# A value product as Strassen's seven block products over pairs of 384 tokens, in three phases via DRAM

## The chip, the cores and the metric

The kernel runs on one core of one Trainium2 chip. The metric is the device time of one execution in microseconds (us), and the lower it is the better. The core's engines are TensorE (PE in the profile, with its weight loads as PEld), VectorE (DVE), ScalarE (ACT), GpSimd (POOL) and SyncE (SP, which issues the DMAs here).

## What is computed

Three blocks follow one another: causal attention with a cumulative decay, a gated spatial block (the first block, moe1 in the code) and a channel-mixing block (the last block). The change is in the last one:

```python
def _moe2_ref(x, mu_k, mu_r, w_k, w_v, w_r):
    x_prev = concatenate([zeros((B, 1, D)), x[:, :-1, :]], axis=1)
    xk = mu_k * x + (1.0 - mu_k) * x_prev
    xr = mu_r * x + (1.0 - mu_r) * x_prev
    k = np.maximum(xk @ w_k, 0.0)
    v = k * k @ w_v                       # 1024 -> 512, the value product
    r = 1.0 / (1.0 + np.exp(-(xr @ w_r))) # the gates
    return r * v
```

There are 4 x 576 = 2304 tokens, the width is 512 and the inner width 1024.

## The kernel before, in words

Every product runs in float32r with operands split in two: a high part (hi, a ScalarE copy to float32r) and the rest (lo, one VectorE subtraction, `split_lo`, line 66). A product of two numbers is then three matmuls, hi x hi, hi x lo and lo x hi, summed in PSUM (`gemm3`, line 355). The weights come as 64-bit words, and `convert` (lines 71 to 88) makes two float32r tiles of them with ScalarE and VectorE passes.

The code is written for a scheduler that runs a timeline model when the program is built: it orders the instructions of each engine by priority (the order of writing) among those that are ready in the model. The order in each queue is thus fixed when the chip runs it; every engine, and SP with its DMAs, takes its instructions in that order. `after(late, early)` adds an edge for that order alone.

Attention (`attn_pair`) and the first block (`moe1`, lines 359 to 465) overlap: `attention_until` interleaves them. The first block's stages are called v, u, sg (the gates ga, split into gh and gl) and o; o leaves y, which lines 464 and 465 store to DRAM twice, in `ydram[0]` as it is and in `ydram[1]` shifted by a token, so that x and x_prev of the last block can be loaded as two rows of one tile.

The last block works on chunks of 512 tokens (the fifth has 256), all stages of a chunk before the next chunk:

- `late(i)` (line 549) loads and converts a slice of w_k (0 to 7), w_r (8 to 11) or w_v (12 to 19).
- `prep(c)` (line 560) loads `yt` and mixes x and x_prev with mu on ScalarE (line 569) and VectorE (line 570), then splits the results, for k (tiles vn0, vn1) and for r (xs0, xs1).
- the k stage (lines 588 to 602): 8 output blocks of 128 rows, each 12 matmuls of 512 columns, then Relu on ScalarE (599), square on VectorE (600), and the split into kh and kl (601, 66). These stay in SBUF.
- `gate(m)` (line 605): 4 blocks, 12 matmuls each, and a Sigmoid on ScalarE.
- the value product, "vo" in the trace (lines 620 to 629): 4 blocks, each 24 matmuls (8 slices of the inner width, 3 matmuls each), then one VectorE pass that multiplies with the gate, and a store to the output.

The PSUM pool `psum1` has all 8 banks (tags sc, tp, acc), and `bank` deals them out in turn. GpSimd works in attention and the first block and has nothing to do in the last block.

Of the kernel before, what the change touches and what calls it, by code (L numbers as in the profile page):

```python
# [37 lines left out]
def fused_kernel(ctx, tc, kqT, vL, s, w_in, g_ln, w_sgT, b_sg, w_out, mu_k, mu_r, w_k, w_v, w_r, out):  # L38
# [52 lines left out]
    psum1 = ctx.enter_context(tc.tile_pool(name="psum1", bufs=3, space=bass.MemoryType.PSUM))  # L91
    ew = ctx.enter_context(tc.tile_pool(name="ew", bufs=1))
    ep = ctx.enter_context(tc.tile_pool(name="ep", bufs=1))
    ap_stack = ExitStack()
    at = ap_stack.enter_context(tc.tile_pool(name="at", bufs=2))
# [9 lines left out]
    wv = [ew.tile([P, KD, FH], F32R, tag=f"wv{i}", name=f"wv{i}") for i in range(2)]  # L105
# [35 lines left out]
    def prologue():  # L141
        st = []
        for i in range(KD + 3):
            if i % 2 == 0:
                raw = ep.tile([P, KD, S], F32, tag="xs0", name=f"sraw{i}")
# [213 lines left out]
    def moe1(b):  # L359
# [5 lines left out]
        xs = [ep.tile([P, KD, S], F32R, tag=f"xs{i}", name=f"xs{i}_{b}") for i in range(2)]  # L365
# [62 lines left out]
        for m in range(KD):  # L428
# [15 lines left out]
            nc.scalar.copy(gs[0][m], ga[:, :S])  # L444
            gs[1].append(ep.tile([P, S], F32R, tag="u", name=f"gl{b}_{m}", bufs=4))
            split_lo(eng, gs[1][m], ga[:, :S], gs[0][m])
        for m in range(KD):
# [19 lines left out]
    exps = []  # L467

# [71 lines left out]
    lw = ctx.enter_context(tc.tile_pool(name="lw", bufs=1))  # L540
    wk = [lw.tile([P, KD, DFF], F32R, tag=f"wk{i}", name=f"wk{i}") for i in range(2)]
    wr = [lw.tile([P, KD, DM], F32R, tag=f"wr{i}", name=f"wr{i}") for i in range(2)]
    wva = [ew.tile([P, KD, FH], F32R, tag=f"wv{i}", name=f"wva{i}") for i in range(2)]
    wvb = [ew.tile([P, NT, S], F32R, tag=f"wsg{i}", name=f"wvb{i}") for i in range(2)]
    wvv = [[wva[i][:, k] for k in range(KD)] + [wvb[i][:, k, :DM] for k in range(KD)] for i in range(2)]
    loads = [(w_k[k * P:(k + 1) * P, j * 512:(j + 1) * 512], [t[:, k, j * 512:(j + 1) * 512] for t in wk]) for j in range(2) for k in range(KD)]
    loads += [(w_r[k * P:(k + 1) * P], [t[:, k] for t in wr]) for k in range(KD)]
    loads += [(w_v[k * P:(k + 1) * P], [t[k] for t in wvv]) for k in range(KF)]
    def late(i):
        src, (hi, lo) = loads[i]  # L550
        raw = lw.tile([P, 512, 2], U32, tag="lraw", name=f"lraw{i}", bufs=2)
        nc.sync.dma_start(out=raw.rearrange("p n c -> p (n c)"), in_=src.bitcast(U32))
        y = lw.tile([P, 512], F32, tag="ltmp", name=f"ly{i}", bufs=4)
        t = lw.tile([P, 512], F32, tag="ltmp", name=f"lz{i}", bufs=4)
        convert(hi, lo, raw, y[:, :512], t[:, :512].bitcast(U32), nc.vector, low=mhalf[:, 0:1])

    CH = 512
    TOK = B * S

    def prep(c):  # L560
        n = min(CH, TOK - c * CH)
        t0 = c * CH
        xx = [[ep.tile([P, KD, S], F32R, tag=t, name=f"x{t}_{c}") for t in r] for r in (("vn0", "vn1"), ("xs0", "xs1"))]
        for k in range(KD):
            yt = lw.tile([P, 2, CH], F32, tag="yt", name=f"yt{c}_{k}", bufs=2)
            nc.sync.dma_start(out=yt[:, :, :n], in_=ydram[:, k, :, t0:t0 + n].rearrange("i p n -> p i n"))
            for r in range(2):
                t = lw.tile([P, CH], F32, tag="ltmp", name=f"lt{c}_{k}_{r}", bufs=4)[:, :n]
                nc.scalar.mul(t, yt[:, 1, :n], mu[:, r, 1, k:k + 1])
                nc.vector.scalar_tensor_tensor(out=t, in0=yt[:, 0, :n], scalar=mu[:, r, 0, k:k + 1], in1=t, op0=ALU.mult, op1=ALU.add)  # L570
                nc.scalar.copy(xx[r][0][:, k, :n], t)
                split_lo(nc.vector, xx[r][1][:, k, :n], t, xx[r][0][:, k, :n])
        return xx

    for c in range((TOK + CH - 1) // CH):
        n = min(CH, TOK - c * CH)
        t0 = c * CH
        if c == 0:
            for i in range(8):
                late(i)  # L580
        xk, xr = prep(c)
        if c == 0:
            for i in range(8, 12):
                late(i)
        kh = [ep.tile([P, S], F32R, tag="xT", name=f"kh{c}_{m}", bufs=8) for m in range(KF)]
        kv = ep.tile([P, KD, S], F32R, tag="v", name=f"kl{c}")
        kk = [kh, [kv[:, m] for m in range(KD)] + [ep.tile([P, S], F32R, tag="u", name=f"kl{c}_{m}", bufs=4) for m in range(KD, KF)]]
        for m in range(KF):
            f = slice(m * P, (m + 1) * P)
            if c == 0:  # L590
                late(12 + m)
            t = ep.tile([P, S + 1], F32, tag="tmp", name=f"lk{c}_{m}", bufs=3)[:, :n]
            acc = bank(f"k{c}_{m}")
            mms = []
            for k in range(KD):
                xh, xl = (x[:, k, :n] for x in xk)
                mms += [(wk[0][:, k, f], xh), (wk[0][:, k, f], xl), (wk[1][:, k, f], xh)]
            gemm3(acc[:, :n], mms)
            nc.scalar.activation(t, acc[:, :n], AF.Relu, scale=1.0 / WS)  # L599
            nc.vector.tensor_tensor(out=t, in0=t, in1=t, op=ALU.mult)  # L600
            nc.scalar.copy(kk[0][m][:, :n], t)
            split_lo(nc.vector, kk[1][m][:, :n], t, kk[0][m][:, :n])
        sg = {}

        def gate(m):
            f = slice(m * P, (m + 1) * P)
            sg[m] = ew.tile([P, S], F32, tag="wc", name=f"sg{c}_{m}", bufs=3)[:, :n]
            acc = bank(f"r{c}_{m}")
            mms = []
            for k in range(KD):  # L610
                xh, xl = (x[:, k, :n] for x in xr)
                mms += [(wr[0][:, k, f], xh), (wr[0][:, k, f], xl), (wr[1][:, k, f], xh)]
            gemm3(acc[:, :n], mms)
            nc.scalar.activation(sg[m], acc[:, :n], AF.Sigmoid, scale=1.0 / WS)

        gate(0)
        for m in range(KD):
            if m + 1 < KD:
                gate(m + 1)
            f = slice(m * P, (m + 1) * P)  # L620
            o = ep.tile([P, S + 1], F32, tag="tmp", name=f"o{c}_{m}", bufs=3)[:, :n]
            acc = bank(f"vo{c}_{m}")
            mms = []
            for k in range(KF):
# [52 lines left out]
```

## Time and profile before

| | us |
|---|---|
| median of 3 runs (706.54 to 709.41) | 708.18 |
| the profiled execution's own time | 706.47 |
| its span, from the first to the last instruction | 704.5 |
| TensorE busy | 668.2 |
| VectorE busy | 438.4 |
| ScalarE busy | 396.0 |
| GpSimd busy | 210.8 |

All rows below come from the one profiled execution. The span is divided into 40 slices of 17.6 us; a digit is the busy share of a slice in tenths. Matmuls are pipelined, so the time of one in a row (0.39 us, say) is longer than the distance from one to the next; the distance is got from the starts of two groups. Attention and the first block take about the first 450 us, the last block the rest.

### The profile page before, as it was taken

The page shows a single profiled execution, that of the slowest core. Times are in us where ns is not written, and L with a number is a line of the kernel's source. Part 1 is how long each engine was busy: PE and PEld are TensorE (multiplying, and loading weights), DVE is VectorE, ACT ScalarE, POOL GpSimd, SP SyncE. Part 2 cuts the span into 40 slices and gives each one's busy share as a digit, 9 for nine tenths or more (in the row PEclk, how much of TensorE's full clock was granted, in tenths as well). Part 3 has the DMA queues.
Part 4 walks back from the last instruction along what each step waited for, and adds up shares of the span by engine and source line. Part 5 has one row for each costly group of instructions (what it writes and reads, how often), then busy time and mean ns, then how long its engine had stood idle before and what let it go on. Part 6 is the DMA issues. An engine that isn't in the chain of part 4 may idle for free.

```text
span 704.5 us, 11476 instructions
## 1 busy us (share of the span) xinstructions
PE 668.2 (95%) x4000; PEld 556.6 (79%) x4000; DVE 438.4 (62%) x996; ACT 396.0 (56%) x899; POOL 210.8 (30%) x219
## 2 busy tenths in 40 slices
PE   2779989999998999999999999999999999999998
PEld 2446767878976889977988899888888888888898
DVE  7876589995578555478743489898744445344140
ACT  5777787874557554368743387598544245234130
POOL 8445555368246258236364140000000000000000
PEclk9979999999999999999999999999999999999999
DMA  7763551542743332743400884753602301100100
GB/s 224 210 194 101 157 153 50 174 146 78 228 149 99 113 84 61 247 122 99 127 18 23 306 301 165 261 175 116 185 25 75 93 13 45 60 16 0 39 22 31
DMA packets 39049, 84.30 MB, mean 120 GB/s; under 512 B 4752, under 2 KB 10384, under 8 KB 38992
## 3 DMA queue, kind: packets, MB, share of 16 engines
q1 hardware_dynamic: 38992, 83.57, 38.1%
q8 instruction: 32, 0.52, 0.3%
q14 instruction: 25, 0.20, 0.1%
HBM read 55.55 MB, written 18.50 MB: 105 GB/s over the span
## 4 chain that ended last, share of the span: by engine, by line
PE 80%; DVE 11%; DMA 3%; ACT 2%; issue 2%; POOL 1%; SPq 0%; DVEq 0%; ACTq 0%; POOLq 0%
PE k L355 14%; PE vo L355 14%; PE pv L326 8%; PE r L355 7%; PE sg L355 7%; PE v L355 6%; PE o L355 6%; PE tp L296 4%; PE sc L247 4%; PE u L355 4%; PE sc L248 3%; DVE st L272 1%; DVE QB L224 1%; DMA lraw<-in_w_k_dram 1%; DMA sraw<-in_w_in_dram 1%
## 5 line engine op out<-in xcount | busy, mean ns | idle before, releaser
L355 PE MATMUL k<-xvn,wk 128*128 128x512 f32 (+1 forms) x480 | 102.0, 373 | 0.3 <-DVE y L461 0.3
L355 PEld LDWEIGHTS k<-xvn,wk 128*128 128x128 f32 x480 | 83.6, 188 | 17.7 <-DVE y L461 0.5
L280 ACT ACTIVATE st<-st,mx 128x128 f32<-128x128 f32 (+4 forms) x124 | 72.3, 585 | 31.2 <-DVE mx L272 29.7
L247 PE MATMUL sc<-ka,qa 128*128 128x512 f32 (+3 forms) x180 | 64.0, 366 | 21.9 <-ACT wv L84 10.6
L272 DVE CUSTOM_DVE_ANT_0 st<-sc,mask 128x512 f32<-128x512 f32 (+3 forms) x124 | 61.0, 501 | 15.6 <-PE sc L248 13.0
L326 PE MATMUL pv<-pt,vf 128*64 128x320 f32 (+4 forms) x448 | 66.7, 375 | 1.3 <-DVE u L485 1.2
L355 PE MATMUL sg<-wsg,vn 128*128 128x288 f32 x448 | 65.0, 298 | 1.2 <-DVE u L485 1.2
L247 PEld LDWEIGHTS sc<-ka,qa 128*128 128x128 f32 x180 | 33.5, 187 | 36.9 <-DVE mx L272 16.0
L355 PEld LDWEIGHTS sg<-wsg,vn 128*128 128x128 f32 x448 | 60.5, 188 | 2.5 <-DVE u L485 1.5
L66 POOL TENSOR_TENSOR KB<-kq,ka 64x576 fp32r<-64x576 f32 x29 | 43.7, 1509 | 50.0 <-ACT ka L225 27.3
L248 PE MATMUL sc<-KB,QB 128*128 128x512 f32 (+3 forms) x180 | 58.2, 336 | 0.2 <-DVE QB_f L224 0.2
L326 PEld LDWEIGHTS pv<-pt,vf 128*64 128x64 f32 x448 | 35.6, 140 | 27.5 <-issue 6.8
L355 PE MATMUL r<-xxs,wr 128*128 128x512 f32 (+1 forms) x240 | 53.4, 373 | 0.0
L66 POOL TENSOR_TENSOR qa<-kq,QB 64x576 fp32r<-64x576 f32 x29 | 43.3, 1493 | 31.0 <-DVE QB L224 17.3
L296 PE MATMUL tp<-ident,st 128*128 128x128 f32 x300 | 48.7, 281 | 3.3 <-ACT st L280 1.7
L599 ACT ACTIVATE lk<-k 128x512 f32<-128x512 f32 (+1 forms) x40 | 22.2, 557 | 51.9 <-PE k L355 48.5
L355 PE MATMUL vo<-kh,wva 128*128 128x512 f32 (+1 forms) x160 | 49.0, 369 | 0.0
L355 PE MATMUL vo<-kh,wvb 128*128 128x512 f32 (+1 forms) x160 | 48.8, 368 | 0.0
L355 PEld LDWEIGHTS r<-xxs,wr 128*128 128x128 f32 x240 | 42.0, 188 | 8.5
L628 DVE SCALAR_TENSOR_TENSOR o<-vo,sg 128x512 f32<-128x512 f32 (+1 forms) x20 | 12.6, 636 | 57.9 <-PE vo L355 57.9
L355 PE MATMUL v<-wv,xs 128*128 128x512 f32 x192 | 48.1, 396 | 0.0
L296 PEld LDWEIGHTS tp<-ident,st 128*128 128x128 f32 x300 | 35.9, 143 | 8.0 <-ACT st L280 2.8
(174 smaller groups left out, 1466.8 us busy)
## 6 DMA issues: line engine op xcount, KB each, us to landing
wc<-wscr SPq DMA_DIRECT2D x24, 512.0 KB
kq<-in_kqT_dram SPq DMA_DIRECT2D x32, 288.0 KB
ydram<-y SPq DMA_DIRECT2D x32, 288.0 KB
yt<-ydram SPq DMA_DIRECT2D x16, 512.0 KB
vf<-in_vL_dram SPq DMA_DIRECT2D x16, 320.0 KB
qa<-QB SPq DMA_DIRECT2D x30, 144.0 KB
ka<-ka SPq DMA_DIRECT2D x30, 144.0 KB
wscr<-wcs SPq DMA_DIRECT2D x8, 512.0 KB
```

The source lines that it names most:

```text
L66: eng.tensor_tensor(out=lo, in0=x, in1=f32(hi), op=ALU.subtract)
L224: (nc.scalar.copy if hd < 2 else nc.vector.tensor_copy)(qb[64:128], kq[64:128])
L247: nc.tensor.matmul(sc[:m, :c1 - c0], qa[:, q], ka[:, c0:c1], start=True, stop=False)
L248: nc.tensor.matmul(sc[:m, :c1 - c0], qb[:, q], kb[:, c0:c1], start=False, stop=True)
L272: nc.vector.tensor_tensor_reduce(out=st[:, c0:c1], in0=sc[:, :n], in1=mk, op0=ALU.add, op1=ALU.min, scale=-SCALE, scalar=mx[:, 0:1] if ci ...
L280: e = nc.scalar.activation(st[:, :w], st[:, :w], AF.Exp, bias=mx[:, last:last + 1], scale=-1.0, accum_out=sm[:, 4 * hh + i % 4:4 * hh + i ...
L296: nc.tensor.transpose(tp[:, c:c + P], st[:, j * P:(j + 1) * P], ident)
L326: nc.tensor.matmul(acc[64 * a:64 * a + 64, o:n], vf[:, a, kk], pt, start=(kk == 0), stop=(kk == nk - 1))
L355: nc.tensor.matmul(acc, a, w_, start=(i == 0), stop=(i == n - 1))
L599: nc.scalar.activation(t, acc[:, :n], AF.Relu, scale=1.0 / WS)
L628: nc.vector.scalar_tensor_tensor(out=o, in0=acc[:, :n], scalar=1.0 / WS, in1=sg[m], op0=ALU.mult, op1=ALU.mult)
```

## The change

The last block no longer runs chunk by chunk but in three phases over all tokens: k, r, v. What passes between them goes through DRAM, in two new tensors: `kdram` (the squared Relu, float32) and `gdram` (the gates).

- Phase k: for each chunk `mixed(c, 0, ...)` mixes x for k alone; `dense` is the same 12 matmuls for a block; two blocks share a tile `t`, VectorE squares it in one pass over 2 x 512 elements, and SP stores it to `kdram`. Nothing is split. Beside it, a list `todo` converts w_r (`late(8)` to `late(11)`) and makes the left factors of w_v: `left(g)` builds, for each half g of the slices, four blocks, the sums s1, s2, s4 and a difference, and splits seven factors into `wvs[g]`.
- Phase r: `mixed(c, 1, ...)` for the gates, `dense`, Sigmoid, a store to `gdram`. The first right factors of the value product are made in its last two chunks.
- Phase v: three pairs of 384 tokens (2 x 384 = 768 = PW). The product of a 2 x 2 block matrix (w_v: output half by inner half) with a 2 x 2 block matrix (squared k: inner half by token half) is formed by seven block products instead of eight. `rights(p)` loads the pair's `kr` tiles (4 DMAs of 768 KB, one buffer for each g) and makes 7 x 2 factors with 8 differences and 14 splits, into 12 slots of 2 x 2 x 384 that are used in turn (`factor`). `product` runs 24 matmuls of 384 columns into a PSUM tile of two banks; products 6, 7 and 4 are added onto what tile a holds, 3 onto tile b. Copies r1, r2, r5 of partial sums are taken by ScalarE between the products, and `block` adds such a copy, multiplies with the gate (loaded from `gdram`) and stores, on VectorE and SP.
- ydram is stored once, with a leading zero row for each batch, and x_prev is read at an offset of one in the same tile; a chunk that crosses a batch is mixed in two segments.
- Pools are moved: `xs` and `wv` become one tile each in a pool `low` that stays; the other tiles of the first block's pools are given back ahead of phase v (`unit1.close()`), the attention pool and those of the phases lie on the right side; `banks1.close()` gives the PSUM banks to `psum2` (4 buffers of two banks) for phase v.
- `last_gate`: the first mix of chunk 0 is ordered behind the last gate copy of the first block.

The core of the diff:

```diff
-    ydram = dram.tile([2, KD, P, B * S], F32, tag="ydram", name="ydram")
+    ydram = dram.tile([KD, P, B, S + 1], F32, tag="ydram", name="ydram")
+    kdram = dram.tile([2, 2, P, 2, B * S], F32, tag="kdram", name="kdram")
+    gdram = dram.tile([2, P, 2, B * S], F32, tag="gdram", name="gdram")
...
-            for i in range(2):
-                nc.sync.dma_start(out=ydram[i, m, :, b * S:(b + 1) * S], in_=y[:, 1 - i:1 - i + S])
+            nc.sync.dma_start(out=ydram[m, :, b], in_=y)
...
+    def mixed(c, r, pool, hold=None):
...
+        for k in range(KD):
+            yt = pool.tile([P, CH + 2], F32, tag="yt", name=f"yt{r}_{c}_{k}", bufs=2 if pool is lk else 4)
...
+            nc.sync.dma_start(out=yt[:, :n + len(segs)], in_=ydram[k].rearrange("p b s -> p (b s)")[:, t0 + t0 // S:t0 + n + t0 // S + len(segs)])
+            for d, (s0, s1) in enumerate(segs):
+                i = nc.scalar.mul(t[:, s0:s1], yt[:, s0 + d:s1 + d], mu[:, r, 1, k:k + 1])
+                if hold is not None:
+                    after(i, hold)
+                nc.vector.scalar_tensor_tensor(out=t[:, s0:s1], in0=yt[:, s0 + d + 1:s1 + d + 1], scalar=mu[:, r, 0, k:k + 1], in1=t[:, s0:s1],
+                                               op0=ALU.mult, op1=ALU.add)
+            last[0] = nc.scalar.copy(xx[:, 0, k, :n], t)
+            split_lo(nc.vector, xx[:, 1, k, :n], t, xx[:, 0, k, :n])
...
+    x = mixed(0, 0, lk, last_gate[0])
+    unit1.close()
+    vw = ctx.enter_context(tc.tile_pool(name="vw", bufs=1, reuse_waits="tile"))
+    kp = kstack.enter_context(tc.tile_pool(name="kp", bufs=1, reuse_waits="tile"))
...
+    for c, (t0, n) in enumerate(TILES):
+        nxt = mixed(c + 1, 0, lk) if c + 1 < len(TILES) else mixed(0, 1, lk)
+        for hg in range(4):
+            t = kp.tile([P, 2, CH], F32, tag="t", name=f"k2_{c}_{hg}", bufs=2)[:, :, :n]
+            for i in range(2):
+                acc = dense(f"k{c}_{hg}_{i}", wk, x, 2 * hg + i, n)
+                nc.scalar.activation(t[:, i], acc, AF.Relu, scale=1.0 / WS)
+            nc.vector.tensor_tensor(out=t, in0=t, in1=t, op=ALU.mult)
+            nc.sync.dma_start(out=kdram[hg // 2, hg % 2][:, :, t0:t0 + n], in_=t)
+            if (c or hg > 1) and todo:
+                todo.pop(0)()
+        x = nxt
...
+    def rights(p, hold=None):
...
+            k = va.tile([P, 2, 2, PW], F32, tag=f"kr{g}", name=f"kr{p}_{g}")
+            for h in range(2):
+                nc.sync.dma_start(out=k[:, h], in_=kdram[h, g][:, :, p * PW:(p + 1) * PW])
...
+        for q in (1, 5, 6, 2, 7, 3, 4):
+            for g in range(2):
+                b11, b12, b21, b22 = kr[g]
+                if q == 1:
+                    make(1, g, b11)
+                elif q == 5:
+                    sub(b11, b12, b11)
+                    make(5, g, b11)
...
+                else:
+                    sub(b21, b21, t2[g])
+                    make(4, g, b21)
+                yield x
...
+    def product(ps, xs, p, start=False):
+
+        for c in range(2):
+            f = slice(c * P, (c + 1) * P)
             mms = []
...
+            for w, x in zip(wvs, xs):
+                for k in range(2):
+                    wh, wl, xh, xl = w[:, p - 1, 0, k, f], w[:, p - 1, 1, k, f], x[p][:, 0, k], x[p][:, 1, k]
+                    mms += [(wh, xh), (wh, xl), (wl, xh)]
+            for i, (l, r) in enumerate(mms):
+                nc.tensor.matmul(ps[:, c, :HW], l, r, start=(start and i == 0), stop=(i == len(mms) - 1), skip_group_check=True)
...
+        product(a, xs, 1, True)
+        copy(r1, a)
+        product(b, xs, 5, True)
+        copy(r5, b)
+        product(a, xs, 6)
+        copy(r2, a)
+        product(c, xs, 2, True)
+        block(0, 0, c, r1)
+        product(a, xs, 7)
+        block(1, 1, a, r5)
+        product(b, xs, 3)
+        block(0, 1, b, r2)
+        product(a, xs, 4)
+        block(1, 0, a, None)
```

## Rows read from the trace of the kernel before

**Rows 1.** The page: busy time by engine, and the span in 40 slices.
```profile
PE 668.2 (95%) x4000; PEld 556.6 (79%) x4000; DVE 438.4 (62%) x996; ACT 396.0 (56%) x899; POOL 210.8 (30%) x219
...
PE   2779989999998999999999999999999999999998
...
DVE  7876589995578555478743489898744445344140
POOL 8445555368246258236364140000000000000000
```

**Rows 2.** The chain of waits in order of time: start us, us, what.
```profile
447.53 7.27 PE k L355 x30
454.80 3.19 PE o L355 x24
...
550.97 10.91 PE vo L355 x48
561.88 22.40 PE k L355 x96
...
672.76 11.31 PE k L355 x96
...
695.48 5.77 PE vo L355 x48
...
701.33 0.42 DVE o L628
```

**Rows 3.** Busy time by stretch: two chunks of the last block.
```profile
core 0: us, PE busy (x) PEld busy (x) DVE busy (x) ACT busy (x) POOL busy (x), PEclk, DMA share, GB/s
561.88:617.32 55.44, 55.44 (x241) 45.16 (x241) 23.25 (x36) 20.43 (x36) 0.00 (x0) 1.00 0.13 42
617.32:672.76 55.44, 55.44 (x242) 45.16 (x242) 18.56 (x32) 16.33 (x32) 0.00 (x0) 1.00 0.05 20
```

**Rows 4.** The timeline of TensorE, 288-column matmuls: start us, us, instructions.
```profile
421.67 14.47 PE L355 MATMUL sg<-wsg,vn 128*128 128x288 f32 x108
435.97 0.29 PE L355 MATMUL o<-gh,wc 128*128 128x288 f32 x1
```

**Rows 5.** Groups by shape, 540 us to the end and 684 us on; timeline (last line).
```profile
L355 PEld LDWEIGHTS k<-xvn,wk 128*128 128x128 f32 x288 | 47.6, 189 | 8.7
L66 DVE TENSOR_TENSOR kl<-lk,kh 128x512 fp32r<-128x512 f32 x16 | 11.1, 692 | 9.6 <-ACT kh L601 9.6
L66 DVE TENSOR_TENSOR kl<-lk,kh 128x256 fp32r<-128x256 f32 x8 | 3.4, 425 | 3.8 <-ACT kh L601 3.8
...
L355 PEld LDWEIGHTS vo<-kh,wva 128*128 128x128 f32 x32 | 5.3, 192 | 0.0
...
498.53 1.90 DVE L66 TENSOR_TENSOR xxs<-lt,xxs 128x512 fp32r<-128x512 f32 x3
```

**Rows 6.** Busy time by earlier stretch, columns as in the third group.
```profile
20.00:60.00 40.00, 31.03 (x180) 20.34 (x179) 32.70 (x78) 29.81 (x79) 20.23 (x14) 0.87 0.60 189
400.00:410.00 10.00, 10.00 (x53) 8.61 (x53) 7.92 (x18) 7.91 (x13) 2.34 (x4) 1.00 1.03 411
410.00:420.00 10.00, 10.00 (x78) 10.00 (x77) 8.97 (x18) 8.07 (x18) 5.72 (x7) 1.00 0.77 249
440.00:450.00 10.00, 8.71 (x54) 7.56 (x54) 10.00 (x20) 6.40 (x10) 0.20 (x2) 1.00 0.55 169
```

**Rows 7.** Waits (waiter, what for: us, times, longest), SP's, its timeline, one load.
```profile
DVE o L628 <- PE vo L355: 57.9, 15, 7.6
...
POOL y L451 <- DMA ydram<-y: 19.7, 3, 9.4
...
SPq L566 <- DVE lt L570: 110.5, 18, 26.1
...
589.14 6.09 SPq L566 DMA_DIRECT2D yt<-ydram  x2
...
417.94 5.63 DMA lraw<-in_w_k_dram
```

More of the change, by code (lines that the diff above doesn't have):

```diff
@@ L364, in moe1 @@
             wcs.append(load_wc(b, c))
-        xs = [ep.tile([P, KD, S], F32R, tag=f"xs{i}", name=f"xs{i}_{b}") for i in range(2)]
+        xs = low.tile([P, 2, KD, S], F32R, tag="xs", name=f"xs_{b}")
+        xs = [xs[:, i] for i in range(2)]
         xq = ep.tile([P, S + 1], F32R, tag="tmp", name=f"xq_{b}", bufs=3)
@@ L546, in fused_kernel @@
-    loads = [(w_k[k * P:(k + 1) * P, j * 512:(j + 1) * 512], [t[:, k, j * 512:(j + 1) * 512] for t in wk]) for j in range(2) for k in range(KD)]
-    loads += [(w_r[k * P:(k + 1) * P], [t[:, k] for t in wr]) for k in range(KD)]
-    loads += [(w_v[k * P:(k + 1) * P], [t[k] for t in wvv]) for k in range(KF)]
+    CH, PW, HW = 512, 768, 384
+    TOK = B * S
+    TILES = [(t0, min(CH, TOK - t0)) for t0 in range(0, TOK, CH)]
+    rstack, kstack = ExitStack(), ExitStack()
+    lw = rstack.enter_context(tc.tile_pool(name="lw", bufs=1, side="right"))
@@ L552, in late @@
         nc.sync.dma_start(out=raw.rearrange("p n c -> p (n c)"), in_=src.bitcast(U32))
[L553 to L563, printed above, removed]
-        for k in range(KD):
[L565 to L572, printed above, removed]
-        return xx
@@ L575, in fused_kernel @@
[L575 to L593, printed above, removed]
-            mms = []
[L595 to L624, printed above, removed]
-                kx = [t[k][:, :n] for t in kk]
-                mms += [(wvv[0][k][:, f], kx[0]), (wvv[0][k][:, f], kx[1]), (wvv[1][k][:, f], kx[0])]
-            gemm3(acc[:, :n], mms)
-            nc.vector.scalar_tensor_tensor(out=o, in0=acc[:, :n], scalar=1.0 / WS, in1=sg[m], op0=ALU.mult, op1=ALU.mult)
-            nc.sync.dma_start(out=out[m].rearrange("p b s -> p (b s)")[:, t0:t0 + n], in_=o)
@@ new lines, in dense @@
+    def dense(name, w, x, m, n):
+        acc = bank(name)
+        f = slice(m * P, (m + 1) * P)
+        mms = []
+        for k in range(KD):
+            xh, xl = (x[:, i, k, :n] for i in range(2))
+            mms += [(w[0][:, k, f], xh), (w[0][:, k, f], xl), (w[1][:, k, f], xh)]
+        gemm3(acc[:, :n], mms)
+        return acc[:, :n]
+    for i in range(8):
+        late(i)
+    x = mixed(0, 0, lk, last_gate[0])
+    unit1.close()
+    vw = ctx.enter_context(tc.tile_pool(name="vw", bufs=1, reuse_waits="tile"))
@@ new lines, in fused_kernel @@
+    todo = [lambda i=i: late(i) for i in range(8, 12)]
+    for g in range(2):
+        it = left(g)
+        todo += [lambda it=it: next(it)] * 7
+    for c, (t0, n) in enumerate(TILES):
+        nxt = mixed(c + 1, 0, lk) if c + 1 < len(TILES) else mixed(0, 1, lk)
+        for hg in range(4):
+            t = kp.tile([P, 2, CH], F32, tag="t", name=f"k2_{c}_{hg}", bufs=2)[:, :, :n]
+            for i in range(2):
+                acc = dense(f"k{c}_{hg}_{i}", wk, x, 2 * hg + i, n)
[5 more added lines that the diff above has]
+        x = nxt
@@ new lines, in fused_kernel, with factor @@
+    kstack.close()
+    ry = rstack.enter_context(tc.tile_pool(name="ry", bufs=1, side="right", reuse_waits="tile"))
+    va = ctx.enter_context(tc.tile_pool(name="va", bufs=1, reuse_waits="tile"))
+    slots = [0]
+    def factor(name):
+        i = slots[0] % 12
+        slots[0] += 1
+        if i < 7:
+            return va.tile([P, 2, 2, HW], F32R, tag=f"xf{i}", name=name)
+        if lowx[i - 7] is None:
+            if i < 9:
+                t = low.tile([P, 2, 2, 2, HW], F32R, tag="wv", name=f"lowx{slots[0]}")
+                lowx[0:2] = [t[:, j] for j in range(2)]
+            else:
+                t = low.tile([P, 3, 2, 2, HW], F32R, tag="xs", name=f"lowx{slots[0]}")
+                lowx[2:5] = [t[:, j] for j in range(3)]
+        return lowx[i - 7]
@@ new lines, in fused_kernel @@
+    x0 = None
+    for c, (t0, n) in enumerate(TILES):
+        nxt = mixed(c + 1, 1, ry) if c + 1 < len(TILES) else None
+        if c == 2:
+            it = rights(0, last[0])
+        if c == 3:
+            for _ in range(3):
+                x0 = next(it)
+        if c == 4:
+            for _ in range(4):
+                x0 = next(it)
+        for h in range(2):
+            g = va.tile([P, 2, CH], F32, tag="g", name=f"g{c}_{h}", bufs=2)[:, :, :n]
+            for i in range(2):
+                acc = dense(f"r{c}_{h}_{i}", wr, x, 2 * h + i, n)
+                nc.scalar.activation(g[:, i], acc, AF.Sigmoid, scale=1.0 / WS)
+            nc.sync.dma_start(out=gdram[h][:, :, t0:t0 + n], in_=g)
+        x = nxt
```

126 lines of the change are left out of this document (112 added, 14 removed).

## The prediction

> **What bounds the kernel now.** I read the page first: TensorE is busy 95% of the span and its slices stay at 9 from the seventh on, while VectorE thins out over the last third and GpSimd does nothing there [rows 1]. Busy alone does not prove a bound, so the chain of waits in order of time comes next: from 447.5 us to 701.3 us it holds nothing but TensorE's k, r and vo products (and the last 24 of o), one starting where the other ends [rows 2]. The stretches agree: a chunk of 512 tokens takes 55.44 us, TensorE is busy in all of it, VectorE in 18.6 to 23.3 us and ScalarE in 16.3 to 20.4 us of it, at a granted clock of 1.00 (2.4 GHz) [rows 3]. So in the last 250 us time is matmuls, and an edit there pays if it removes matmul time and still feeds TensorE. The profiled execution took 706.47 us (span 704.5 us and 1.97 us around it); the median of the runs is 708.18 us, 1.71 us above it. I sum against 706.47 us and add 1.71 us at the end.
>
> **Matmul time.** The value product was 96 matmuls a chunk (4 blocks of 8 slices of K, 3 each), 480 in all. A 512-column one runs at 10.91 us / 48 = 227.3 ns, a 256-column one at 5.77 / 48 = 120.2 ns [rows 2]. One full chunk is 2 x 10.91 = 21.82 us; four of them and the short one, 2 x 5.77 = 11.54 us, make 98.8 us (the first chunk's pieces lie among others; I count it like the rest). After: 3 pairs x 7 products x 2 column halves x 2 groups x 2 slices x 3 = 504 matmuls of 384 columns. No row has 384 columns; the nearest lie on both sides. The middle of 120.2 and 227.3 is 173.7 ns; the line from the 288-column sg matmuls ((435.97 - 421.67) / 108 = 132.4 ns [rows 4]) to 227.3 gives 173.1; with the k rows as ends (11.31 / 96 = 117.8 and 22.40 / 96 = 233.3 [rows 2]) it is 175.6. I take 174 ns: 87.7 us, 11.1 us less (10.3 to 11.6). The k and r products keep number and width: 100.9 and 50.5 us, only regrouped.
>
> Smaller matmuls mean more weight loads for each column, 504 instead of 480. A load lasts 189 to 192 ns by its rows, yet 256-column matmuls with a load each follow one another every 118 to 120 ns [rows 2, 5], so loads overlap the matmul before and no 189 ns floor is added. The Trainium skill ("TensorE: Matmul & The Clock Gate", Part 3, what overlaps and what doesn't) says that a weight load overlaps matmuls in flight only when their row groups differ, and (LDWEIGHTS) that it takes 128 / 1.2 GHz, 107 ns; all matmuls here use the full array. By that rule 24 more loads would cost 2.6 us and the gain in columns would be 11.5 us at 2.4 GHz, about 9 us in all (my estimate). The trace disagrees with the rule, since 107 ns of load in series with 107 ns of 256 columns is 214 ns and the rows show 120; the rows decide.
>
> **The end.** Now: a 0.42 us pass over 256 columns, then two stores, and the span ends 2.75 us after the pass [rows 2]. After: one pass over 2 x 384 elements. VectorE rows of 692 ns for 512 and 425 ns for 256 give 1.04 ns an element [rows 5], so 0.96 us, and two stores of 192 KB instead of one of 128 KB that follows others. I charge 0.9 us (0.5 to 1.5).
>
> **The junction with the first block's end.** From 440 to 450 us TensorE is idle 1.29 us while VectorE is busy all of the 10 us [rows 6]: it mixes chunk 0 for both k and r there and converts w_r. After, only k's mix of chunk 0 remains (4 instead of 8 pairs of pass and split), held behind the last gate copy, and w_r moves into the k phase. The gates lose a competitor; the mix starts later: gate copy near 438.5 us (sg ends at 436 us [rows 4], then two passes and the copy), four steps of about 1.4 us each and a lead of 2.9 us, so ready near 446 us, before o's 96 matmuls (12.8 us from 436 us) are through. I take 0.5 us gained (1.3 gained to 2 lost). Ahead of it, 16 of the 32 stores to ydram on SP's queue go; the only one who shows a wait for them is GpSimd's memset of y, 19.7 us in 3 waits [rows 7], off the path: nothing, with 2 us either way, since another program also lays out memory and order anew.
>
> **Phase k.** VectorE adds up to about 78 us in 101 us: passes start every 0.605 us for 512 elements ([rows 5]: three in 1.90 us), 0.87 for 768, 1.14 for 1024. Mixes 27 us (five of 8 passes of 512, one of 256 columns), squares 20.6 (18 of 1024), w_r 7.3 (12 of 512), the parts of w_v 23 (16 to convert, 14 splits, 8 sums). It hides under 100.9 us of matmuls. The new kdram stores wait on SP for the square, and 8 PSUM banks (22 us of matmuls) stand between.
>
> **k to r.** The pools of r lie where k's weights lay, so the first r chunk that is mixed in this phase can load only after the last k matmul: no row shows a lone 256 KB load; a crowded 512 KB one took 5.63 us [rows 7]. From half of that to all of it, then 6.5 us for four mixing steps, is 9 to 12 us against 11.2 us of r's first chunk plus some for the later slices. Nothing to 1.5 us; I take 0.5.
>
> **Phase v.** A pair needs 22 VectorE passes (14 splits, 8 differences) and 7 for the blocks: 29 x 0.87 = 25.2 us against 168 x 0.174 = 29.2 us of TensorE. The first pair has 11 of its passes done in phase r, so it is 66 us of 88 us: enough, but the thinnest margin in the kernel. The kr buffer is single: pair 1's 3.15 MB can load only when pair 0's last differences are done, about 10 us into the phase (the slots of product 1 must come free, at 4.2 us). At the 411 GB/s that the trace reaches and at 249 GB/s in a mixed stretch [rows 6] that is 7.7 to 12.6 us, so it lands by 20 to 25 us, and pair 1's first product is due at 29.2 us, then one every 4.2 us; its q4 factors are due at 54 us and ready near 41 us. Pair 2 loads from 41 us, lands by 51 to 56 us, due at 58.4 us. Each accumulation onto a bank that ScalarE or VectorE has just read has another product (4.2 us) between. Waits of the new order on in-order queues: 0 to 6 us in all, for no row shows them; VectorE waited 58 us for TensorE at the gate pass alone [rows 7], and the chain holds no wait of TensorE there [rows 2], so I stay near the low end: 1.0 us.
>
> **The sum.** 706.47 - 11.1 + 0.9 - 0.5 + 0.5 + 1.0 = 697.3 us, and with 1.71 us 699.0 us. Bounds together: 694 to 704.
>
> **Rivals.** (a) Fed late in part: ScalarE's copy r2 and VectorE's block (1,1), each due within 4.2 us, stand in order behind a split that still waits for kr; each pair boundary and the k-r junction lose 3 us or so. 699 + 8 = 707 us. For: VectorE at 86% in steady state, one kr buffer; against: the bounds above end on time. (b) Slower: SP takes DMAs in order, and its own waits are long (110 us for VectorE's passes at the yt loads [rows 7]). If the kr loads of pair p+1 stand behind the last stores of pair p, they start when the pair ends: three of four quarters must come (6 to 9.5 us), with some 2 us of lag (512 KB took 5.63 us [rows 7], 1.3 us at 411 GB/s; I take half of the rest) and 2 us for the first splits (2 x 0.87), 10 to 13 us twice, and a stretch of idle TensorE also brings a lower granted clock, as 20 to 60 us shows (busy 31 of 40 us, 0.87: part at 2.4, part at 1.2 GHz) [rows 6]. 699 + 23 = 722 us. It decides if kr is issued later than 15 us into a pair. Against: loads for the next chunk were issued well ahead of its use in the old phase (yt from 589 us for a chunk that starts at 617 us [rows 7]). (c) The saving is not there: matmuls of 384 columns run at the load's 190 ns, 95.8 us, 707 us. Against: rows at 256 and 288 columns. (d) The first half or the junction also gains, as the lighter VectorE load could let it: 694 us.
>
> **Chances.** Forecast 0.67, (a) 0.13, (b) 0.10, (c) 0.04, (d) 0.06. A measurement of this kernel can tell 0.5% from no change, that is 704.6 to 711.7 us. Faster is the forecast and (d), 0.73; same (a) and (c), 0.17; slower (b), 0.10. The range goes from 694 to 708 us: it takes in the bounds, (a) and (c), and leaves out (b) and the tails.
>
> **What would show it.** Right: product groups of 24 in 4.2 us; no TensorE wait over 1 us from the k phase to the end; kr of pair 1 issued about 10 us into phase v. Wrong: TensorE waits for a split (ScalarE or VectorE) at a pair boundary, SP's wait of the kr loads on an out store, a granted clock below 1.00 while the last block's products run, 384-column matmuls above 180 ns, or a different time before 440 us.

## The result and the profile after

The changed kernel takes 697.45 us (median of 6 runs, 696.17 to 699.46), the kernel before, run beside it on the same chip, 707.92 us (6 runs, 706.54 to 709.41). The ratio is 0.9854 (95% interval 0.9832 to 0.9875): 10.5 us less, 8.8 to 11.9. The profiled execution after took 699.46 us with a span of 697.7 us, which is the longest of its six; the profiled one before (706.47 us) is not among those six and is shorter than all of them. So the two traces lie only 7.0 us apart, and terms read from a pair of traces must be held against other executions too.

The page of the changed kernel (busy time by engine, and the span in 40 slices of 17.4 us), against [rows 1]:

```profile
PE 658.5 (94%) x4024; PEld 561.7 (81%) x4024; DVE 490.2 (70%) x1041; ACT 419.5 (60%) x940; POOL 211.1 (30%) x219
...
PE   2869989999999999999999998999999999999997
...
DVE  6876589994668655468754378787767768768763
POOL 7455545367335357435455022000000000000000
```

TensorE lost 9.7 us of busy time although it has 24 matmuls more. VectorE gained 52 us, and in the last third its digits went from mostly 3 to 5 to mostly 6 to 8. The chain of the changed kernel in order of time (start us, us, what), against [rows 2]:

```profile
454.65 3.18 PE o L359 x24
457.83 97.85 PE k L359 x466
555.68 50.40 PE r L359 x240
606.08 4.17 PE psa L758 x24
610.25 4.16 PE psb L758 x24
...
685.30 4.00 PE psb L758 x23
...
689.32 0.97 DVE t L783
...
691.68 1.82 DMA out_dram<-t
693.50 0.95 DVE t L781
```

The three phases follow one another without a gap. A product of 24 matmuls of 384 columns lasts 4.16 us, 173.4 ns each, and phase v reaches from 606.08 us to the last product's end at 693.45 us (689.30 plus the last 24 matmuls): 87.4 us. Busy time by stretch (columns as in [rows 3]):

```profile
440.00:450.00 10.00, 10.00 (x77) 10.00 (x76) 7.94 (x14) 4.73 (x9) 0.20 (x2) 1.00 0.25 66
457.83:555.68 97.85, 97.85 (x468) 80.97 (x467) 73.54 (x115) 65.36 (x126) 0.00 (x0) 1.00 0.58 194
555.68:606.08 50.40, 50.40 (x242) 41.59 (x241) 38.42 (x66) 37.46 (x76) 0.00 (x0) 1.00 0.64 225
606.08:689.30 83.22, 83.22 (x482) 83.22 (x481) 59.61 (x67) 33.95 (x43) 0.00 (x0) 1.00 0.55 184
```

TensorE is busy in all of the last block at a granted clock of 1.00 (2.4 GHz); VectorE is busy 75%, 76% and 72% of the phases. The weight loads are busy all of phase v. The waits of TensorE from 400 us to the end of the span are this single one (waiter, what for: us, times, longest), and it is new:

```profile
PE sg L359 <- DVE vn L68: 2.7, 1, 2.7
```

It stands ahead of the last batch's sg product in the first block, before any line of the last block's products runs. Where does it come from? The timeline of ScalarE, first in the kernel before, then in the changed one (start us, us, instruction, in brackets the idle time before it and what ended it):

```profile
400.51 1.28 ACT L477 ACT_TABLE_LOAD   x1
401.81 0.60 ACT L477 ACTIVATE v<-v 128x512 f32<-128x512 f32 x1
404.44 0.66 ACT L73 ACTIVATE ly<-lraw 128x512 f32<-128x512 f32 x1 [2.04 <-DMA lraw<-in_w_k_dram]
...
422.40 0.60 ACT L405 CAST vn<-v 64x512 fp32r<-64x512 f32 x1
```

```profile
404.37 0.66 ACT L75 ACTIVATE ly<-lraw 128x512 f32<-128x512 f32 x1 [2.64 <-DMA lraw<-in_w_k_dram]
405.06 1.28 ACT L482 ACT_TABLE_LOAD   x1
406.35 0.60 ACT L482 ACTIVATE v<-v 128x512 f32<-128x512 f32 x1
...
425.71 0.68 ACT L75 ACTIVATE ly<-lraw 128x512 f32<-128x512 f32 x1 [2.04 <-DMA lraw<-in_w_k_dram]
...
427.51 0.61 ACT L410 CAST vn<-v 64x512 fp32r<-64x512 f32 x1
```

Before, the first gelu of v stands ahead of the pass on the third slice of w_k. After, that pass stands first in ScalarE's queue and waits 2.64 us for its DMA, so the gelu starts 4.5 us later, and the last copy vn that sg needs is 5.1 us later, behind another such pass. The change edits none of these lines (it rewrites `late`, which calls the passes, and the stores to ydram beside them); the program was laid out anew and the order came out another. Which part of the edit turned it is not shown.

### The profile page after: what moved, and what is told of

The parts are those of the page before. It is cut to its first block, busy times and chain, and to the rows that moved or that the text cites. A ratio compares the mean times of both kernels' runs of the same rounds, so it can differ in the third digit from the quotient of the medians.

```text
span 697.7 us, 11759 instructions
## 1 busy us (share of the span) xinstructions
PE 658.5 (94%) x4024; PEld 561.7 (81%) x4024; DVE 490.2 (70%) x1041; ACT 419.5 (60%) x940; POOL 211.1 (30%) x219
## 4 chain that ended last, share of the span: by engine, by line
PE 80%; DVE 9%; DMA 5%; ACT 2%; issue 2%; POOL 1%; SPq 0%; DVEq 0%; ACTq 0%; POOLq 0%
PE k L359 14%; PE sg L359 8%; PE pv L330 8%; PE r L359 7%; PE psa L758 7%; PE o L359 6%; PE v L359 6%; PE tp L300 5%; PE u L359 4%; PE sc L251 4%; PE psb L758 4%; PE sc L252 3%; DMA lraw<-in_w_k_dram 3%; PE psc L758 2%; DVE st L276 1%
## 5 line engine op out<-in xcount | busy, mean ns | idle before, releaser
L359 PE MATMUL k<-x,wk 128*128 128x512 f32 (+1 forms) x480 | 101.4, 372 | 0.0
L359 PEld LDWEIGHTS k<-x,wk 128*128 128x128 f32 x480 | 83.6, 188 | 17.4
L276 DVE CUSTOM_DVE_ANT_0 st<-sc,mask 128x512 f32<-128x512 f32 (+3 forms) x124 | 61.2, 502 | 16.6 <-PE sc L252 12.6
L359 PE MATMUL sg<-wsg,vn 128*128 128x288 f32 x448 | 66.9, 303 | 3.9 <-DVE vn L68 2.7
L359 PEld LDWEIGHTS sg<-wsg,vn 128*128 128x128 f32 x448 | 62.3, 192 | 5.0 <-DVE vn L68 2.9
L359 PE MATMUL r<-x,wr 128*128 128x512 f32 (+1 forms) x240 | 50.6, 372 | 0.0
L359 PEld LDWEIGHTS r<-x,wr 128*128 128x128 f32 x240 | 41.7, 188 | 8.8
L359 PE MATMUL o<-gh,wc 128*128 128x288 f32 x192 | 41.2, 299 | 0.0
L359 PE MATMUL u<-xs,wc 128*128 128x288 f32 x288 | 41.0, 297 | 0.0
L578 ACT ACTIVATE yx<-yt,mu 128x64 f32<-128x64 f32 (+4 forms) x64 | 30.6, 534 | 17.2 <-DMA yt<-ydram 16.3
L359 PEld LDWEIGHTS v<-wv,xs 128*128 128x128 f32 x192 | 35.0, 188 | 6.9
```

The costliest lines, as they stand in the source:

```text
L276: nc.vector.tensor_tensor_reduce(out=st[:, c0:c1], in0=sc[:, :n], in1=mk, op0=ALU.add, op1=ALU.min, scale=-SCALE, scalar=mx[:, 0:1] if ci ...
L359: nc.tensor.matmul(acc, a, w_, start=(i == 0), stop=(i == n - 1))
L578: i = nc.scalar.mul(t[:, s0:s1], yt[:, s0 + d:s1 + d], mu[:, r, 1, k:k + 1])
```

## The experiments

Each kernel is the changed one with an edit, unless it says otherwise. Times are medians. The kernel before ran beside all of them: at 707.35 us beside the kernels with eight products, with seven of eight slices, with the first order edge and with kr late; at 707.42 beside the changed kernel run again, the gelus first, and 21 and 42 passes more; at 708.5 beside the other four. Ratios are to it, with their 95% interval.

**What does the saving come from: seven products, or the phases?** First, eight block products in the same three phases:

```diff
-        product(a, xs, 1, True)
...
-        block(1, 0, a, None)
+        for h, c in ((0, 0), (1, 0), (0, 1), (1, 1)):
+            a = psum2.tile([P, 2, 512], F32, tag="ps", name=f"ps{h}{c}_{p}", bufs=4)
+            product(a, xs, 1 + 2 * h, 1 + c, True)
+            product(a, xs, 2 + 2 * h, 3 + c)
+            block(h, c, a, None)
```

> The changed kernel with eight block products instead of seven: the same three phases, DRAM tensors, pairs of 384 tokens and matmul width, but four factors on each side (no sums, no differences, 8 splits a pair instead of 14), two products added into each of four PSUM tiles. Theory (matmul time decides): 72 more matmuls of 173.4 ns, +12.5 us on 697.45 us, so 710 us (707 to 712), in spite of 14 fewer VectorE passes a pair. Rival (the regrouping in phases brought the gain, the number of products did not matter): at most 700 us. Third possibility (the regrouping costs, as well as brings): well above 712 us.

710.72 us, ratio 1.0054 (1.0029 to 1.008). Its chain of waits:

```profile
604.63 99.86 PE ps L733 x576
```

99.86 us for 576 matmuls, 173.4 ns each, 12.5 us above the seven products' 87.4. With eight products the phases are 3.4 us slower than the kernel before by the medians, 3.8 by the ratio, so all of the gain is the eighth product that isn't formed. The terms for those 3.4 to 3.8 us, added up and not tested one by one: the value product with 384 columns instead of 512 (99.86 against 98.8) and the longer end (+1.0, below); that leaves 1.3 to 1.7 for the junction (below). The kernel also has fewer splits and no differences; that relief gave no time that shows.

The mirror of it, on the kernel before: seven of the eight slices of the inner width, the last one left out of the value product.

```diff
-            for k in range(KF):
+            for k in range(KF - 1):
```

> The kernel before, with seven of the eight slices of the inner width in the value product (the eighth slice is left out, so part of the sum is missing from the output): 12 matmuls a chunk less. Theory (the old last block is bound by TensorE alone): 4 x 12 x 227.3 ns + 12 x 120.2 ns = 12.4 us off 707.92 us, 695.6 us (694 to 697). Rival (VectorE, ScalarE or the loads of the next chunk come next and give part of it back): 700 us or more.

694.71 us, ratio 0.9837 (0.9806 to 0.9868): 12.6 us less by the medians, 11.5 (9.3 to 13.7) by the ratio, where 12.4 us of matmuls went. For a cut of this size the old last block was bound by TensorE alone, as [rows 2, 3] had it.

**Is it ScalarE's order that costs the junction?** First only the last two slices of w_k were put behind the last copy vn:

```diff
+        if behind is not None:
+            for i in (i0, i1):
+                after(i, behind)
...
-        convert(hi, lo, raw, y, t.bitcast(U32), nc.vector, low=mhalf[:, 0:1])
+        convert(hi, lo, raw, y, t.bitcast(U32), nc.vector, low=mhalf[:, 0:1], behind=last_vn[0] if i in (6, 7) else None)
```

> The changed kernel, with ScalarE's two first passes on the last two slices of w_k ordered behind the last vn copy of the first block; nothing else moves on TensorE. Theory (the 2.7 us that TensorE's sg waits for vn at 426 to 429 us come from ScalarE's order: a pass that waits for a slice of w_k stands ahead of the vn copy): the wait goes, 2 to 3 us less, 694.5 to 695.5 us. Rival (that wait is one execution's slow transfer, or the next wait takes its place): 697.45 us within 1 us.

697.48 us, ratio 0.9867 (0.9837 to 0.9898): a miss. The wait of sg was 1.5 us; the gelus were still behind the third slice. So the edge was put on slices 2 to 7 (counted from 0), each behind one of the five copies vn of the last batch, and run beside the changed kernel itself:

```diff
+            vns.append(nc.scalar.copy(vn[0][:m, t], v[:m, t]))
...
+        convert(..., behind=vns[-5:][min(i - 2, 4)] if 1 < i < 8 else None)
```

> The changed kernel unaltered, as the neighbour of the next three on one chip. Expected at its median of 697.5 us (696 to 699.5). In its trace the wait of TensorE for VectorE ahead of the last batch's sg product, 2.7 us in the first trace of this kernel, shows again with 1.5 to 3 us, and no wait of TensorE after 440 us.

> On the changed kernel, ScalarE's first two passes on the slices 2 to 7 of w_k stand in its order behind the five copies vn of the last batch of the first block (slice 2 behind the first copy, slice 6 and 7 behind the last), so that the gelus of v come ahead of the passes that wait for a slice's DMA. Theory (the first half lost 1.3 to 3.6 us because those passes stand ahead of the gelus): the wait of sg for VectorE (1.5 to 2.7 us) falls below 0.5 us and the time to 694.5 to 696.5 us. Rival (the junction is bound by the arrival of the weights, not by ScalarE's order): the wait moves into the k product behind the last o, where a slice of w_k comes late, and the time stays at 697.5 +- 1 us.

The changed kernel: 698.4 us (696.08 to 699.99), ratio 0.9869 (0.9846 to 0.9891), with a wait of 1.9 us. With the edges: 695.87 us (694.54 to 696.97), ratio 0.9836 (0.9814 to 0.9857), and no wait of TensorE from 400 us on. Its chain of waits:

```profile
422.07 14.85 PE sg L362 x112
...
449.73 3.18 PE o L362 x24
452.91 17.26 PE k L362 x74
```

The wait is gone, so the theory holds in place. The median fell by 2.5 us, which fits its size, but the intervals of the two ratios overlap, so the times alone do not show it. The weights' arrival does not bound this place: no wait of TensorE came in its stead. Of the kernels that form the whole product this one and the last one below are the fastest.

**How near is phase v to its limits?** First kr late (pairs are counted from 0 here, as in the prediction): the loads of pairs 1 and 2 ordered behind the last store of the pair before.

```diff
-                nc.sync.dma_start(out=k[:, h], in_=kdram[h, g][:, :, p * PW:(p + 1) * PW])
+                d = nc.sync.dma_start(out=k[:, h], in_=kdram[h, g][:, :, p * PW:(p + 1) * PW])
+                if p:
+                    after(d, last_store[0])
...
+                last_store[0] = nc.sync.dma_start(...)
```

> The changed kernel, with the kr loads of pairs 1 and 2 ordered on SP's queue behind the last store of the pair before. Theory (the early reload is what keeps TensorE fed; its price was worked out as 10 to 13 us at each of two pair boundaries): 697.45 + 20 to 26 us, 717 to 723 us, with TensorE waiting for splits at two places and a granted clock below 1.00 there. Rival (the factors in the 12 slots and the products under way cover the load anyway): 697.45 us within 2 us.

732.14 us, ratio 1.0357, 34.7 us above the changed kernel or 17 us a pair boundary: the mechanism of rival (b), dearer than I had it. The longest wait of TensorE, the loads in the chain, and the second boundary in stretches:

```profile
PE psa L761 <- ACT xv L607: 17.2, 2, 9.6
```

```profile
639.66 6.05 DMA kr<-kdram
...
683.67 8.07 DMA kr<-kdram
```

```profile
681.00:690.00 9.00, 0.16 (x1) 0.00 (x0) 0.96 (x1) 0.12 (x1) 0.00 (x0) 0.63 0.94 305
690.00:699.00 9.00, 7.18 (x19) 5.77 (x20) 8.18 (x10) 6.68 (x9) 0.00 (x0) 0.50 0.60 233
```

TensorE stood 7.6 and 9.6 us for the first quarters of kr. Then, for 9 us at each boundary, it ran 20 matmuls, which are 3.5 us of work at 173.4 ns each. Two things go together there: ScalarE and VectorE make the first factors one after another in the time in which they are wanted (VectorE is busy 8.2 of the 9 us), and after the pause TensorE went on at a granted clock of 0.50 (1.2 GHz), so that its matmuls were busy 7.2 of the 9 us. The run does not tell the two apart.

Next VectorE's margin. It does some of the fourteen split subtractions of a pair twice (the same result written again), seven, all fourteen, or three of them:

```diff
             split(x[g][q], v, hold)
+            if g == 0:
+                split_lo(nc.vector, x[g][q][:, 1], v, x[g][q][:, 0])
```

> On the changed kernel, VectorE does seven of the fourteen split subtractions of a pair twice (the factors of the first half of the slices), the same result written again: about 0.95 us a pass, 20 us in all three pairs, 15 of them in phase v, on top of 59.6 us busy in its 83 us. Theory (VectorE has room in phase v, 75 of 87 us busy): the waits stay below 1 us each and the time is 697.5 to 701 us. Rival (VectorE's order is tight at each product, so any extra pass shows): each factor comes 0.95 us later where TensorE wants it, 7 x 3 x 0.95 = 20 us, 705 to 717 us.

> On the changed kernel, VectorE does all fourteen split subtractions of a pair twice, the same result written again: 42 more passes of 0.95 us, 40 us, some 30 of them in phase v: 59.6 + 30 = 90 us busy where TensorE needs 87.4 us. Theory (VectorE's load becomes the bound once it passes TensorE's): 3 to 15 us longer, 700 to 712 us, with waits of the products for VectorE's xv in pairs 2 and 3. Rival (TensorE's order is fed far enough ahead that the sum over the phase doesn't matter): within 1 us of 697.5 us.

> On the changed kernel, VectorE does three of the fourteen split subtractions of a pair twice (products 1, 2 and 3, first half of the slices), the same result written again: 9 more passes, 8.6 us. With seven of fourteen twice (21 passes) it took 12.3 us longer. Theory (there is a point from which it shows: pair 2's kr loads may be issued some 7 us later than in the changed kernel before its first product comes late): 697.5 to 700 us. Rival (every extra pass shows, in proportion): 12.3 x 9 / 21 = 5.3 us, 701.5 to 704.5 us.

| passes more in all | VectorE's time more, us | median us | ratio (interval) |
|---|---|---|---|
| 0 | 0 | 698.4 | 0.9869 (0.9846 to 0.9891) |
| 9 | 8.6 | 699.85 | 0.9871 (0.984 to 0.9903) |
| 21 | 20 | 710.67 | 1.0046 (1.0025 to 1.0067) |
| 42 | 40 | 713.77 | 1.0096 (1.0065 to 1.0127) |

In the medians nine passes cost nothing, and twenty-one eat the whole gain. (The second column is passes times 0.95 us.) My theory for seven of fourteen (room by the sum: 75 of 87 us) was wrong, and the rival's number was met, but its reason (each pass shows) was not: nine passes do not show in proportion, which would be 5.3 us. In the trace of the nine the time from the end of o to the end of the span is 241.3 us where the changed kernel has 239.9, with this one wait of TensorE in the last block:

```profile
PE psa L760 <- DVE t L785: 1.1, 1, 1.1
```

It stands in the last pair, where product 3 came ahead of product 7, so that product 4 followed product 7 on the same tile and waited for the pass between them: another order again, not VectorE's load. Forty-two passes missed their theory too (700 to 712 us), with waits of 4.8 and 4.5 us already in pair 1. There is a point, and it lies below the full load of VectorE. Why, the kernel with 21 passes more shows. SP's timeline and the chain (the kr loads of pair 2), a pass of VectorE, the waits of TensorE, and the stretches after them:

```profile
645.68 4.68 SPq L693 DMA_DIRECT2D kr<-kdram  x4
```

```profile
647.30 1.83 DVE xv L68 x2
649.18 0.52 SPq L693
...
649.75 8.69 DMA kr<-kdram
...
658.73 0.95 DVE xv L68
659.68 0.88 DVE t L785
660.60 8.44 PE psa L760 x47
```

```profile
659.60 0.95 DVE L785 SCALAR_TENSOR_TENSOR t<-psa,r 128x768 f32<-128x768 f32 x1
```

```profile
PE psb L760 <- DVE xv L68: 5.3, 1, 5.3
PE psa L760 <- DVE t L785: 3.5, 2, 2.4
```

```profile
673.40:678.83 5.43, 0.15 (x1) 0.00 (x1) 5.43 (x8) 1.00 (x2) 0.00 (x0) 0.79 0.12 43
678.83:685.17 6.34, 6.34 (x24) 6.34 (x25) 5.16 (x6) 0.00 (x0) 0.00 (x0) 0.64 0.38 124
```

In the changed kernel the loads of pairs 1 and 2 were issued here (SP's timeline):

```profile
611.10 2.69 SPq L693 DMA_DIRECT2D kr<-kdram  x4
...
641.55 0.56 SPq L693 DMA_DIRECT2D kr<-kdram  x1
...
644.10 2.01 SPq L693 DMA_DIRECT2D kr<-kdram  x3
```

The last of pair 2 ends 40.0 us after the start of phase v (646.1 - 606.1). With 21 passes more it ends 46.4 us after it (650.36 - 603.96), and 17.3 us after the pair before began (29.1 us a pair). The chain has the loads behind VectorE's splits of the old kr. From the last issue to 660.6 us it is 10 us: 8.69 us of load, a copy, a split, and then the pass of block (1,1) of pair 1 (t<-psa,r), which stands in VectorE's order behind that split. Product 4 of pair 1 adds onto the tile that this pass reads, so it waits 2.4 us; this is the wait that rival (a) named. From there VectorE has no lead left (busy 5.43 of 5.43 us), product 5 of pair 2 (tile b) waits 5.3 us, and the 23 matmuls behind that pause take 6.34 us at a granted clock of 0.64 instead of 4.0. The third wait, 1.1 us, is again the order of product 3 and 7 in the last pair. Waits of 8.8 us and about 2.3 us of clock make 11.1 of the 12.3 us. So in this run the margin of phase v was the release of the single kr buffer, and VectorE's passes are what released it. With nine passes more the last issue of pair 2 came 40.6 us after the start of the phase, only 0.6 us later than in the changed kernel: the point lies between there and 46.4 us, and no run is nearer to it.

**GpSimd idles there; can it take the eight differences of a pair?** Alone, and with seven of fourteen splits done twice:

```diff
+    def gsub(out, a, b):
+        nc.gpsimd.tensor_tensor(out=out, in0=a, in1=b, op=ALU.subtract)
...
             for g in range(2):
+                sub = gsub
```

> On the changed kernel, the eight differences of a pair are formed by GpSimd instead of VectorE (24 passes of 768 elements; by its rows of 1.43 us for 576 elements some 1.9 us each where VectorE takes 0.95). Theory (TensorE waits for nothing after 450 us, so relief of VectorE buys nothing and GpSimd's slower pass costs nothing while factors are early): 696.5 to 699 us. Rival (a factor's chain sets the release of kr, and the slower differences delay the next pair's loads): 8 x 0.95 us later a pair, 701 to 712 us.

> The eight differences of a pair on GpSimd and seven of the fourteen split subtractions done twice by VectorE, so VectorE has one pass a pair less than in the changed kernel, and the chain of the factors is longer. Theory (the 12.3 us of the run with seven twice came from VectorE's time): 697 to 701 us. Rival (they came from the longer way to the last use of kr, whichever engine it runs on): 708 to 716 us.

708.52 us, ratio 0.9999 (0.998 to 1.0018), and 720.77 us, ratio 1.0181 (1.0154 to 1.0207). The first is within the rival's numbers, the second above them: moving 8 of VectorE's 29 passes of a pair to GpSimd costs some 9 us, most of the gain. In the first, phase r ends 1.4 us late after a wait of the r product, and phase v takes 95.3 us instead of 87.4; TensorE's waits from 450 us on are short, 5.2 us in all, but the granted clock from 637.5 to 666.6 us is 0.88. The longer way to kr's release is the rival's reason; another stands beside it, and the runs do not separate the two. The timelines of VectorE and of GpSimd in the first of the two:

```profile
627.09 0.94 DVE L68 TENSOR_TENSOR xv<-t,xv 128x768 fp32r<-128x768 f32 x1
627.96 0.94 DVE L787 SCALAR_TENSOR_TENSOR t<-psc,r 128x768 f32<-128x768 f32 x1
628.94 1.62 DVE L788 TENSOR_TENSOR t<-t,gt 128x768 f32<-128x768 f32 x1
630.64 2.44 DVE L68 TENSOR_TENSOR xv<-kr,xv 128x768 fp32r<-128x768 f32 x1
```

```profile
621.98 1.84 POOL L688 TENSOR_TENSOR t<-kr 128x768 f32<-128x768 f32 x1
...
627.25 2.49 POOL L688 TENSOR_TENSOR kr<-kr 128x768 f32<-128x768 f32 x1 [0.90 <-DVE xv L68]
629.82 2.45 POOL L688 TENSOR_TENSOR t<-kr 128x768 f32<-128x768 f32 x1
```

A VectorE pass with two SBUF operands that falls beside a GpSimd difference takes 1.62 to 2.6 us instead of 0.95, and the difference takes 2.5 us instead of 1.84; the excess is about the time that the other still needs to its end (an estimate from the starts and ends shown). The pass at 627.96 us, one operand of which is in PSUM, takes its 0.94 us with GpSimd busy beside it. The Trainium skill ("SBUF — State Buffer", Who interferes with whom) says just this: a VectorE instruction with two SBUF inputs contends with a GpSimd instruction that reads SBUF, and one with at most one SBUF input does not, outside the modes that use two ports. The traces here agree.

**The end.** The kernel with the gelus first, and the last block's pass made in two halves:

```diff
-                nc.vector.scalar_tensor_tensor(out=t, in0=ps[:, :, :HW], scalar=1.0 / WS, in1=g, op0=ALU.mult, op1=ALU.mult)
+                for i in range(2):
+                    nc.vector.scalar_tensor_tensor(out=t[:, i], in0=ps[:, i, :HW], scalar=1.0 / WS, in1=g[:, i], op0=ALU.mult, op1=ALU.mult)
```

> On the kernel with the gelus first (695.9 us): the pass on a pair's last block is made in two halves of 384 columns, so that the first half is multiplied and stored while TensorE still forms the second. Theory (the pass stands on the way to the end, 0.95 us, then a store of 1.82 us): 0.4 to 1 us less between TensorE's last matmul and the end, 695 to 695.6 us. Rival (the stores share SP's order and arrive no sooner): no change, 695.9 +- 0.7 us.

695.93 us, ratio 0.9828 (0.9803 to 0.9854): not to be told from 695.87. Its timeline of VectorE:

```profile
689.53 1.02 DVE L786 SCALAR_TENSOR_TENSOR t<-psa,gt 128x384 f32<-128x384 f32 x2 [2.22 <-DMA out_dram<-t]
```

The first half didn't start while TensorE formed the second; both halves start after the last matmul (689.49 us), and the profile names the landing of the store before as what released them. In the changed kernel, too, it names that store, and the pass starts at 693.50 us, as here just behind the last matmul (693.45 us); what held the first half stays open. From the last matmul to the end of the span it is 3.8 us instead of 4.3: half a microsecond, at the lower end of the theory, and too small for the medians.

## Why the prediction was right, step by step

| step | predicted us | measured us |
|---|---|---|
| value product | -11.1 (-10.3 to -11.6) | -11.4 |
| the end | +0.9 (0.5 to 1.5) | +1.0 |
| junction | -0.5 (-1.3 to +2) | +0.2 and +1.2 over all executions of two sets (estimate, below); +3.6 in the two profiled executions |
| k to r | +0.5 (0 to 1.5) | 0 |
| waits in phase v | +1.0 (0 to 6) | 0 |
| sum | -9.2 | -10.2 and -9.2 by these terms; -10.5 and -9.0 by the medians of the two sets |

**The forecast, 699.0 us, was 1.5 us above the median of 697.45.** By its terms the two profiled executions add up: -11.4 + 1.0 + 3.6 is -6.8, and they differ by 7.0 us. That the medians differ by more is the choice of executions: another of the changed kernel has a span of 694.3 us, 3.4 us shorter, all of it ahead of the end of o (454.44 against 457.83 us). My 1.71 us from the profiled execution to the median belonged to the kernel before alone. Part of the nearness is luck: 1.5 us of waits that I charged did not come, and the junction took back half of that or all of it, by the estimates below. The line "Bounds together: 694 to 704" is also no sum of the terms: their ends, with 2 us either way for layout, reach from 693.8 to 710.9 us, and nothing in the working gives 704.

**The value product** was right: 384-column matmuls follow one another every 173.4 ns (I took 174), below the 188 ns that a weight load shows by its record, and the step gained 11.4 us. Rival (c), 190 ns a matmul, is out. The Trainium skill ("TensorE: Matmul & The Clock Gate", Part 3, what overlaps and what doesn't) has loads overlap matmuls in flight only where the row groups differ. By that rule I had estimated about 9 us gained; the trace does not agree.

**The end** was right: 4.25 us from the last matmul to the end of the span instead of 3.25.

**The junction** came out with the wrong sign, within my bounds. What I named did come: from 440 to 450 us TensorE has no idle time, where it had 1.29 us [rows 6]. I had left 2 us either way for an order laid out anew, but I named no place. It was ScalarE's order, with a DMA wait in front of a gelu: all nine traces with that order have the wait of sg, 0.8 to 2.7 us, and the two of the old last block (before, and seven of eight slices) have none. Its size in the time is less sure. At the end of o with 14 k matmuls done, the nine traces lie at 453.5 to 459.8 us, mean 456.7; the two old ones at 457.98 and 458.85 us with 30 done, less 16 x 0.233 us, mean 454.7. That is 2.0 us, but from two traces on one side, and the spread is as wide as 6 us.

More executions can be used. From the end of o to the end of the span the changed kernel takes 239.87 and 239.86 us in its two traces; the kernel before takes 246.52 us, and 3.73 more for the 16 matmuls. If that holds in executions without a trace (an estimate), their spans give the end of o. In the first set it is 456.0 us (mean of 6) against 455.8 for the kernel before (6, with 2.0 us taken off their times for what lies around the span). Beside the kernel with the gelus first it is 456.6 (5) against 455.4 (13). So the change lost some 0.2 to 1.2 us here. The kernel with the gelus first has 454.0 us (5) against the same 455.4: with that order the junction gains some 1.4 us, all that I had allowed it. With these terms the sum closes within 0.3 us of the medians. Rival (d), a gain in the first half, did not come.

**k to r and phase v** cost nothing; I had 1.5 us. The first r chunk was there on time (the chain has no gap at 555.68 us), VectorE needed 59.6 of 83.2 us where I had 66 of 88, and the kr loads of pair 1 went out 5.0 to 7.7 us into the phase, not at 10. Rival (a), late in part, did not come in the changed kernel; its wait came with 21 passes more.

**Rival (b)** had the right mechanism, and too low a price. It decided, I wrote, if kr is issued later than 15 us into a pair; in the changed kernel pair 2's last load left 10.9 us into pair 1, with 21 passes more 17.3 us, and then TensorE waited. But the first wait was (a)'s, for block (1,1) behind a split, so 15 us is not confirmed as (b)'s point. The price at the pair's very end was 17 us a boundary, not 10 to 13: the step counted the load and the first splits, and gave the lower clock no time; the runs showed 9 us more in which TensorE did 3.5 us of matmuls, at a granted clock of 0.50 and at the pace of the early factors.

**The 66 of 88 us** were a true sum and a poor measure of safety: I called it enough with the thinnest margin in the kernel, and 20 us more, 15 of them in this phase and so by sum still 90% of TensorE's time, cost 12 us.

## What to carry to other kernels

In a stretch where TensorE alone bounds, each product that isn't formed is worth its matmuls at the rate between the rows of the neighbouring widths, and here the extra additions were free while they hardly moved the release of a single buffer: ask of such a buffer when its next load must be issued, not what share of the engine is busy. An edit to one block can change an engine's order ahead of that block, when a program lays out all queues anew: compare the order of the untouched part first, and pin what waits for a DMA behind what doesn't. An idle GpSimd is no free VectorE: beside two-operand passes from SBUF it slows both.

## What the runs showed of the hardware

- GpSimd and VectorE hold each other up: VectorE's pass over 768 elements with both operands in SBUF took 0.95 us alone and up to 2.6 us beside a GpSimd difference, which itself took 1.84 us alone and 2.5 us beside such passes; with one operand in PSUM VectorE's pass kept 0.94 us.
- Weight loads with a record of 188 ns each stand beside matmuls that follow one another every 173.4 ns; busy time of the loads is then the whole stretch (83.22 of 83.22 us), and a load's record is no floor for the spacing of matmuls.
- A pause of 5.3 us of TensorE was followed by 23 matmuls in 6.34 us at a granted clock of 0.64, 1.6 times their time at 1.00; a pause of 9.6 us was followed by 9 us at 0.50.
